# Decode attention on one core: VectorE products and sums over half heads instead of quarters, softmax totals once per four heads

## The chip, the cores and the metric

The kernel runs on one core of one Trainium2 chip. The metric is the device time of the whole program in microseconds (us), lower is better, as the median of several executions. The profile is one further execution; its span is about 1.8 us shorter than the time, so spans are compared with spans and times with times.

## The reference

One decoding step for four sequences: a layer norm, attention of 32 heads over the last 2048 positions of a cache, a gated FFN, and a sum.

```python
B, D, H, Dh, F = 4, 640, 32, 192, 1536            # bf16; W = 2048 positions of 8192
xn = layernorm(x)
q  = (xn @ wq) per head                           # one query row per sequence and head
p  = softmax(q . k[:, :, -2048:, :] * Dh ** -0.5)
o  = p . v[:, :, -2048:, :]
out = x + concat(o) @ wo + (silu(xn @ w1) * (xn @ w3)) @ w2
```

Each head needs 3.15 MB of K and 3.15 MB of V and uses each element once. That is 201 MB of the 223 MB which the kernel reads.

## The kernel before

K of one head lies in SBUF as 128 partitions (32 groups of positions x 4 sequences) x 64 positions x 192. A score is a dot product of length 192. The kernel forms it in three steps per *quarter* of a head (16 of the 64 positions): VectorE multiplies K by the query, TensorE adds six slices of 32 columns with an identity matrix into PSUM, VectorE sums the last 32. Then come a maximum over the head (VectorE, a TensorE transpose, VectorE again), exp on ScalarE, a masked copy `z` of the weights, and the PV matmuls.

```python
    def mult(u):                                   # u counts quarters: h, g = u // 4, u % 4
        pr = ppool.tile([P, JQ, Dh], BF16, tag="pr")
        nc.vector.tensor_tensor(out=pr[:], in0=kts[h][:, g * JQ:(g + 1) * JQ, :],
                                in1=qbc[...].to_broadcast([P, JQ, Dh]), op=ALU.mult)
        # ... (cut: bookkeeping)
    def adder(u):
        # ... (cut: the tiles ps and pr)
        for kk in range(NK):                       # 6 matmuls, 512 columns
            nc.tensor.matmul(ps[:], lhsT=idb[:], rhs=pr[:, :, kk * DD:(kk + 1) * DD], ...)
    def reduce_quarter(u):
        nc.vector.tensor_reduce(out=scs[h][:, g * JQ:(g + 1) * JQ], in_=pss.pop(u)[:], ...)
    def ge_tot(h):                                 # softmax total of one head, every head
        nc.tensor.matmul(po[sl, Dh:Dh + 1], lhsT=tot_w[...], rhs=rsums.pop(h)[:], ...)
```

The program is written as a table of (slot, phase, step). Within an engine the program records the instructions in exactly this order, and the traces show one whose input is late holding up those behind it: in the changed kernel the last 12 sums on TensorE start at 511.04 us, though their product is ready at 505.66, because a PV ahead of them waits for its z until 509.63. One slot is one quarter.

```python
    ends = {H - 2: (NU - 1, NU), H - 1: (NU + 3, NU + 4)}   # PV and fp32 sum of the last two heads
    for h in range(H):
        u0, ul = h * GQ, h * GQ + GQ - 1
        if h >= KBUFS: add((h - KBUFS + 1) * GQ, 0, load_k, h)
        if h < H - 2:  add(u0 + 2, 0, load_v, h)
        for u in range(u0, ul + 1):
            add(u, 1, mult, u); add(u + 1, 2, adder, u); add(u + 1, 8, reduce_quarter, u)
        add(ul + 1, 9, chain_lmax, h)               # VectorE: maximum per partition
        add(ul + 2, 3, chain_tr, h)                 # TensorE: transpose
        add(ul + 2, 4, chain_gmax, h)               # VectorE: maximum per sequence
        add(ul + 3, 3, chain_bc, h)                 # TensorE: broadcast; ScalarE: exp
        add(ul + 3, 4, chain_z, h)                  # VectorE: z
        add(ul + 4, 5, ge_tot, h)
        v, m = ends.get(h, (u0 + L, u0 + L + 1))
        add(v, 7, pv, h); add(m, 7, ge_sum, h)      # TensorE: PV; fp32 sum of its parts
        # ... (cut: once per four heads, the reciprocal of the totals and the turning of the output)
    # ... (cut: after K of head 31 the queue still loads V 30, V 31, w2 pieces, wo, w2 pieces)
```

## Time and profile before

| | value | where it is read |
|---|---|---|
| time | 525.69 us (525.55 to 526.71) | executions |
| span of the profiled run | 523.8 us | page |
| loads | 222.96 MB, load queue 99.2% of 16 engines | page, queue table |
| VectorE (DVE) / TensorE (PE) busy | 340.9 / 361.8 us | page |
| VectorE idle until a K tile came | 104.0 us | groups |

First the page of the kernel before: the span, then the span in 40 slices (DMA in tenths of full use, and what it moved).

```profile
span 523.8 us, 4820 instructions
...
DMA  9999999999999999999999999999999999999996
GB/s 389 422 443 425 433 431 432 428 433 432 430 435 428 437 418 446 424 437 426 434 434 429 432 434 429 435 427 435 425 437 434 427 437 431 430 434 425 441 418 275
```

The DMA row reads 9 (90% or more) in 39 of 40 slices and the rate is flat near 432 GB/s in the middle. No compute engine passes 70%. So the middle of the run is bound by bytes, and only the two ends can move.

The groups of the same kernel: line, engine, operation, output<-inputs, count | busy us, mean ns of one | idle us of the engine just before, and what ended it.

```profile
L277 DVE TENSOR_TENSOR pr<-kt,qbc 128x3072 bf16<-128x3072 bf16 x128 | 223.5, 1746 | 104.0 <-DMA kt<-in_A_k_cache_dram 104.0
L296 DVE TENSOR_REDUCE sc<-ps 128x16 f32<-128x512 f32 x128 | 87.1, 681 | 2.7 <-PE ps L288 2.6
...
L332 DVE TENSOR_TENSOR z<-ex,mask_b 128x256 bf16<-128x256 bf16 x32 | 13.5, 423 | 38.6 <-ACT ex L324 38.6
```

VectorE waits 104.0 us for K tiles, 3.3 us per head: it is ahead of the loads. Next, the chain that ended last, in order of time (start us, us, what).

```profile
489.68 30.66 DMA w<-in_B_w_dram
520.38 0.76 PE acc L264 x8
```

The end hangs on the last pieces of w2. Finally the end of the run in the timeline (start us, us, engine, line, operation).

```profile
496.99 1.76 DVE L277 TENSOR_TENSOR pr<-kt,qbc 128x3072 bf16<-128x3072 bf16 x1 [4.05 <-DMA kt<-in_A_k_cache_dram]
...
506.11 1.75 DVE L277 TENSOR_TENSOR pr<-kt,qbc 128x3072 bf16<-128x3072 bf16 x1
...
509.41 0.69 DVE L296 TENSOR_REDUCE sc<-ps 128x16 f32<-128x512 f32 x1 [0.95 <-PE ps L288]
...
512.82 0.42 DVE L332 TENSOR_TENSOR z<-ex,mask_b 128x256 bf16<-128x256 bf16 x1 [1.47 <-ACT ex L324]
...
513.30 2.71 PE L340 MATMUL o_ps<-vt,z 128*8 128x384 bf16 x32 [0.24 <-DVE z L332]
...
518.65 0.38 DVE L369 STREAM_TRANSPOSE oT<-og 128x192 bf16<-128x192 bf16 x1
...
520.38 0.71 PE L264 MATMUL acc<-w,hT 128*4 128x320 bf16 x8 [0.19 <-DMA w<-in_B_w_dram]
```

The last K tile is multiplied from 496.99 us, the last product ends at 507.86, the last sum at 510.10, the last z starts at 512.82, the last attention output is turned at 518.65, and the last w2 matmuls wait for DMA until 520.38. The work of the last head and the last load end within about 0.2 us of each other (its projection ends at 519.21 + 0.98 = 520.19).

### The profile page before, as it was taken

To read this page: it belongs to the slowest core of one execution; us is meant where nothing else is said; L and a number is where in the kernel's file an instruction comes from. 1 tells how busy PE (TensorE), PEld (TensorE's weight loads), DVE (VectorE), ACT (ScalarE), POOL (GpSimd) and SP (SyncE) were. 2 spreads that over 40 slices of the span, in tenths; PEclk is the share of its full clock that TensorE was granted. 3 is DMA by queue.
4 is the path that set the end of the run, shared out by engine and by line. 5 is a ranking of instruction groups with operands and counts; after the bars stand their busy time and mean duration, and the time that the engine had idled before them with its cause. 6 is when DMAs were issued, how large, how long until landed. Compare 5 with 4: busy or idle time off the path is not lost.

```text
span 523.8 us, 4820 instructions
## 1 busy us (share of the span) xinstructions
PE 361.8 (69%) x2336; PEld 75.9 (14%) x1643; DVE 340.9 (65%) x413; ACT 55.8 (11%) x176; POOL 5.6 (1%) x12
## 2 busy tenths in 40 slices
PE   0965866887668776667547768586686876675685
PEld 0100111121111111111111111111111111111122
DVE  3268853687656767577646877466667766667671
ACT  2111111111001110101100111001101110011111
POOL 4000000000000000000000000000000000000000
PEclk9979886898878998789997988889878898889988
DMA  9999999999999999999999999999999999999996
GB/s 389 422 443 425 433 431 432 428 433 432 430 435 428 437 418 446 424 437 426 434 434 429 432 434 429 435 427 435 425 437 434 427 437 431 430 434 425 441 418 275
DMA packets 11904, 223.26 MB, mean 426 GB/s; under 512 B 1332, under 2 KB 1608, under 8 KB 3052
## 3 DMA queue, kind: packets, MB, share of 16 engines
q1 hardware_dynamic: 11868, 222.96, 99.2%
q8 instruction: 15, 0.25, 0.2%
q14 instruction: 5, 0.04, 0.0%
q10 hardware_dynamic: 16, 0.01, 0.0%
HBM read 222.96 MB, written 0.01 MB: 426 GB/s over the span
## 4 chain that ended last, share of the span: by engine, by line
DMA 60%; PE 20%; DVE 15%; ACT 3%; issue 1%; SPq 1%
DMA kt<-in_A_k_cache_dram 44%; PE ps L288 11%; DMA w<-in_B_w_dram 11%; DVE pr L277 10%; DMA vt<-in_A_v_cache_dram 5%; PE po L361 4%; PE qps L243 3%; DVE sc L296 2%; ACT ex L324 1%; DVE z L332 1%; DMA x_sb<-in_A_x_dram 1%; PE mt L318 1%; ACT L324 0%; ACT negm L321 0%; PE mt L305 0%
## 5 line engine op out<-in xcount | busy, mean ns | idle before, releaser
L288 PE MATMUL ps<-pr,idb 128*128 128x512 bf16 x768 | 214.7, 422 | 137.6 <-DVE pr L277 137.5
L277 DVE TENSOR_TENSOR pr<-kt,qbc 128x3072 bf16<-128x3072 bf16 x128 | 223.5, 1746 | 104.0 <-DMA kt<-in_A_k_cache_dram 104.0
L296 DVE TENSOR_REDUCE sc<-ps 128x16 f32<-128x512 f32 x128 | 87.1, 681 | 2.7 <-PE ps L288 2.6
L340 PE MATMUL o_ps<-vt,z 128*8 128x384 bf16 x1024 | 60.5, 380 | 0.2 <-DVE z L332 0.2
L361 PE MATMUL po<-o_sb,sel_w 128*32 128x192 f32 x128 | 49.2, 518 | 0.6 <-ACT o_sb L343 0.6
L340 PEld LDWEIGHTS <-z 128*8 128x8 bf16 x1024 | 26.2, 95 | 98.8 <-issue 89.2
L332 DVE TENSOR_TENSOR z<-ex,mask_b 128x256 bf16<-128x256 bf16 x32 | 13.5, 423 | 38.6 <-ACT ex L324 38.6
L343 ACT COPY o_sb<-o_ps 128x384 f32<-128x384 f32 x32 | 15.3, 478 | 196.9 <-PE o_ps L340 196.9
L313 ACT ACTIVATE gneg<-gmax 1x128 f32<-1x128 f32 x32 | 9.8, 308 | 162.8 <-DVE gmax L310 162.8
L305 PEld LDWEIGHTS mt<-idf,lmax 128*1 128x1 f32 x32 | 3.2, 101 | 127.5 <-issue 125.5
L361 PEld LDWEIGHTS po<-o_sb,sel_w 128*32 128x32 f32 x128 | 13.8, 130 | 29.4 <-issue 27.9
L288 PEld LDWEIGHTS <-idb 128*128 128x128 bf16 x124 | 12.0, 97 | 39.3 <-issue 32.8
L318 PEld LDWEIGHTS mt<-ones_ff,gneg 1*128 1x128 f32 x64 | 9.6, 186 | 47.1 <-issue 43.7
L243 PE MATMUL qps<-wt,xnT 128*128 128x512 bf16 x59 | 14.9, 412 | 0.1
L318 PE MATMUL mt<-ones_ff,gneg 1*128 1x1 f32 x64 | 12.3, 259 | 0.7 <-ACT gneg L313 0.7
L321 ACT COPY negm<-mt 128x1 f32<-128x1 f32 x32 | 5.1, 159 | 70.4 <-PE mt L318 70.4
L310 DVE TENSOR_REDUCE gmax<-mt 1x4 f32<-1x128 f32 x32 | 8.8, 274 | 5.8 <-PE mt L305 5.8
L348 PEld LDWEIGHTS po<-rsum,tot_w 128*32 128x32 f32 x64 | 4.4, 108 | 51.5 <-ACT ex L324 35.4
L249 DVE CAST qbc<-qps 128x512 bf16<-128x512 f32 x6 | 3.8, 684 | 11.7 <-PE qps L243 11.7
L324 ACT ACTIVATE ex<-sc,negm 128x64 bf16<-128x64 f32 x32 | 11.1, 348 | 1.0
L305 PE MATMUL mt<-idf,lmax 128*1 128x128 f32 x32 | 10.9, 340 | 0.0
L199 PE MATMUL xnT_ps<-idb,xn 4*128 4x4 bf16 x5 | 0.4, 178 | 13.4 <-DVE xn L194 13.4
(74 smaller groups left out, 84.4 us busy)
## 6 DMA issues: line engine op xcount, KB each, us to landing
kt<-in_A_k_cache_dram SPq DMA_DIRECT2D x32, 3072.0 KB, 19.1
vt<-in_A_v_cache_dram SPq DMA_DIRECT2D x32, 3072.0 KB, 25.5
wo_t<-in_A_wo_dram SPq DMA_DIRECT2D x8, 960.0 KB, 20.7
wt<-in_A_wq_dram SPq DMA_DIRECT2D x2, 3072.0 KB
w<-in_B_w_dram SPq DMA_DIRECT2D x1, 1920.0 KB
wt<-in_A_wq_dram SPq DMA_DIRECT2D x1, 1536.0 KB, 19.5
w<-in_B_w_dram SPq DMA_DIRECT2D x1, 1536.0 KB
w<-in_B_w_dram SPq DMA_DIRECT2D x2, 640.0 KB
```

What stands on the lines that cost most here:

```text
L243: nc.tensor.matmul(qp[:], lhsT=xnT[:, kc].rearrange("p a b -> p (a b)"), rhs=wq_rows[kc][:, (c0 + i) * QC:(c0 + i + 1) * QC], start=(kc == ...
L277: nc.vector.tensor_tensor(out=pr[:], in0=kts[h][:, g * JQ:(g + 1) * JQ, :], in1=qbc[:, h * Dh:(h + 1) * Dh].unsqueeze(1).to_broadcast([P, ...
L288: nc.tensor.matmul(ps[:], lhsT=idb[:], rhs=pr[:, :, kk * DD:(kk + 1) * DD], start=(kk == 0), stop=(kk == NK - 1))
L296: nc.vector.tensor_reduce(out=scs[h][:, g * JQ:(g + 1) * JQ], in_=pss.pop(u)[:], axis=AX.X, op=ALU.add)
L305: nc.tensor.transpose(out=mt[0:1, 0:P], in_=chs[h][0][:], identity=idf[:])
L313: nc.scalar.activation(out=gneg[:], in_=gmax[:].unsqueeze(1).to_broadcast([1, PB, B]), func=ACTF.Copy, scale=-SCALE)
L318: nc.tensor.matmul(mt[:, P:P + 1], lhsT=gneg[:].rearrange("o p b -> o (p b)"), rhs=ones_ff[:], start=True, stop=True)
L324: nc.scalar.activation(out=ex[:], in_=scs.pop(h)[:], func=ACTF.Exp, bias=negm[:, 0:1], scale=SCALE, accum_out=rsum[:])
L332: nc.vector.tensor_tensor(out=z[:], in0=ex[:].unsqueeze(2).to_broadcast([P, NJ, B]), in1=mask_b[:].unsqueeze(1).to_broadcast([P, NJ, B]), ...
L340: nc.tensor.matmul(o_ps[c * CT:c * CT + 2 * B, :], lhsT=z[:, 2 * jj:2 * jj + 2, :], rhs=vt[:, 2 * jj:2 * jj + 2, :], start=(jj < 4), stop= ...
L343: nc.scalar.copy(out=o_sb[:], in_=o_ps[:])
L361: nc.tensor.matmul(po[sl, 0:Dh], lhsT=sel_w[:, par].rearrange("p a b -> p (a b)"), rhs=o_sb[:, par * Dh:(par + 1) * Dh].rearrange("p (r i) ...
```

## The change

The intent: save a fixed cost per VectorE instruction by doing the products and sums in half as many, twice as long; let TensorE do 12 sums in a row; form the softmax totals once per four heads with one matmul; and take the preparation of the FFN's input off the path to the first query. One sum now takes twice the PSUM (128x1024 fp32 instead of 128x512), and other PSUM pools are merged. The core of the diff (cut: the moved FFN preparation, constants moved to GpSimd, merged PSUM pools):

```diff
-    PBUFS: int = 4,
+    PBUFS: int = 2,
@@ mult
-        pr = ppool.tile([P, JQ, Dh], BF16, tag="pr")
-        nc.vector.tensor_tensor(out=pr[:], in0=kts[h][:, g * JQ:(g + 1) * JQ, :], ...
+        pr = ppool.tile([P, 2 * JQ, Dh], BF16, tag="pr")
+        nc.vector.tensor_tensor(out=pr[:], in0=kts[h][:, g * JQ:(g + 2) * JQ, :], ...
@@ adder
-        ps = ps_add.tile([P, JQ, DD], FP32, tag="ps")
+        ps = ps_add.tile([P, 2, JQ, DD], FP32, tag="ps")
-        for kk in range(NK):
-            nc.tensor.matmul(ps[:], lhsT=idb[:], rhs=pr[:, :, kk * DD:(kk + 1) * DD],
+        for i in range(2):
+            for kk in range(NK):
+                nc.tensor.matmul(ps[:, i], lhsT=idb[:], rhs=pr[:, i * JQ:(i + 1) * JQ, kk * DD:(kk + 1) * DD],
@@ schedule
-        for u in range(u0, ul + 1):
+        for u in range(u0, ul, 2):
             add(u, 1, mult, u)
-            add(u + 1, 2, adder, u)
-            add(u + 1, 8, reduce_quarter, u)
+            add(u + 2, 2, adder, u)
+            add(u + 2, 8, reduce_pair, u)
-        add(ul + 4, 5, ge_tot, h)
         if h % HG == HG - 1:
+            add(ul + 4, 4, ge_mask, h // HG)        # VectorE product, new
+            add(ul + 4, 5, ge_tot, h // HG)         # one matmul for four heads
             add(ul + 4, 9, ge_rec, h // HG)
```

More of the change, by code (lines that the diff above doesn't have):

```diff
@@ L111 @@
     ps_o = ctx.enter_context(tc.tile_pool(name="ps_o", bufs=2, space=MemoryType.PSUM))
-    ps_m = ctx.enter_context(tc.tile_pool(name="ps_m", bufs=1, space=MemoryType.PSUM))
-    ps_t = ctx.enter_context(tc.tile_pool(name="ps_t", bufs=1, space=MemoryType.PSUM))
     ps_po = ctx.enter_context(tc.tile_pool(name="ps_po", bufs=1, space=MemoryType.PSUM))
@@ L120 @@
     kts, vts, prs, pss, scs, exs, zs = {}, {}, {}, {}, {}, {}, {}
-    wos, o_sbs, rsums, rts, chs, oTs = {}, {}, {}, {}, {}, {}
+    wos, o_sbs, rsums, rws, rts, chs, oTs = {}, {}, {}, {}, {}, {}, {}
     def load_k(h):
@@ L157 @@
     make_identity(nc, idf[:])
-    ones_ff = const.tile([1, 1], FP32, name="ones_ff")
-    nc.vector.memset(ones_ff[:], 1.0)
+    ones_ff = const.tile([P, 1], FP32, name="ones_ff")
+    nc.gpsimd.memset(ones_ff[:], 1.0)
     mask_f = const.tile([P, B], FP32, name="mask_f")
@@ L163 @@
     mask_b = const.tile([P, B], BF16, name="mask_b")
-    nc.vector.tensor_copy(out=mask_b[:], in_=mask_f[:])
+    nc.gpsimd.tensor_copy(out=mask_b[:], in_=mask_f[:])
     rows = const.tile([P, 2 * B], FP32, name="rows")
@@ L170 @@
     tot_w = head.tile([P, NREP, B], FP32, name="tot_w")
-    nc.vector.tensor_copy(out=tot_w[:], in_=mask_f[:].unsqueeze(1).to_broadcast([P, NREP, B]))
+    nc.gpsimd.tensor_copy(out=tot_w[:], in_=mask_f[:].unsqueeze(1).to_broadcast([P, NREP, B]))
     sel_w = const.tile([P, 2, NREP, B], FP32, name="sel_w")
     for par in range(2):
-        nc.vector.tensor_copy(out=sel_w[:, par], in_=rows[:, par * B:(par + 1) * B].unsqueeze(1).to_broadcast([P, NREP, B]))
+        nc.gpsimd.tensor_copy(out=sel_w[:, par], in_=rows[:, par * B:(par + 1) * B].unsqueeze(1).to_broadcast([P, NREP, B]))
     xf = ppool.tile([B, D], FP32, tag="pr")
@@ L194 @@
     nc.vector.tensor_scalar_mul(out=xn[:], in0=xc[:], scalar1=rstd[:, 0:1])
-    xnT_ps = ps_t.tile([P, KC, B], BF16, tag="t")
+    xnT_ps = ps_add.tile([P, KC, B], BF16, tag="ps")
     for kc in range(KC):
@@ L208 @@
     assert D - LB == 5 * LP + LI and F % LE == 0
-    xm = ppool.tile([B, 2, PH, 2], BF16, tag="pr", name="xm")
-    nc.gpsimd.memset(xm[:], 0.0)
-    for i in range(2):
-        nc.vector.tensor_copy(out=xm[:, i, :, i], in_=xn[:, KM * P:LB])
-    xe = ppool.tile([B, 3 + LE, LF], BF16, tag="pr", name="xe")
-    nc.gpsimd.memset(xe[:], 0.0)
-    for g in range(2):
-        b0 = LB + g * 2 * LP
-        nc.vector.tensor_copy(out=xe[:, 0:2, g * CT:g * CT + LP].rearrange("b s (e i) -> b s e i", i=LI),
-                              in_=xn[:, b0:b0 + 2 * LP].rearrange("b (i e s) -> b s e i", e=LE, s=2))
@@ L219 @@
-    nc.vector.tensor_copy(out=xe[:, 2, 0:LP].rearrange("b (e i) -> b e i", i=LI),
-                          in_=xn[:, LB + 4 * LP:LB + 5 * LP].rearrange("b (i e) -> b e i", e=LE))
-    for e in range(LE):
-        nc.vector.tensor_copy(out=xe[:, 3 + e, CT + e * LI:CT + (e + 1) * LI], in_=xn[:, LB + 5 * LP:D])
-    NX = KM + 2
-    xw_ps = ps_t.tile([P, NX + 3 + LE, B], BF16, tag="t", name="xw_ps")
-    for kc in range(KM):
-        nc.tensor.transpose(out=xw_ps[:, kc, :], in_=xn[:, kc:KM * P:KM], identity=idb[0:B, 0:B])
@@ L227 @@
-    for i in range(2):
-        nc.tensor.transpose(out=xw_ps[:, KM + i, :], in_=xm[:, i].rearrange("b r h -> b (r h)"), identity=idb[0:B, 0:B])
-    for i in range(3 + LE):
-        nc.tensor.transpose(out=xw_ps[0:LF, NX + i, :], in_=xe[:, i, :], identity=idb[0:B, 0:B])
-    xw = const.tile([P, NX, NREP, B], BF16, name="xw")
-    nc.vector.tensor_copy(out=xw[:], in_=xw_ps[:, 0:NX, :].unsqueeze(2).to_broadcast([P, NX, NREP, B]))
-    xl = const.tile([LF, 3 + LE, NREP, B], BF16, name="xl")
-    nc.vector.tensor_copy(out=xl[:], in_=xw_ps[0:LF, NX:, :].unsqueeze(2).to_broadcast([LF, 3 + LE, NREP, B]))
@@ L237 @@
     qbc = const.tile([P, H * Dh], BF16, name="qbc")
     for c0 in range(0, NQ, 6):
-        qps = [pool.tile([P, QC], FP32, tag=tag, name="qps")
-               for pool, tag in ((ps_add, "ps"), (ps_add, "ps"), (ps_o, "o_ps"), (ps_o, "o_ps"), (ps_m, "mt"), (ps_t, "t"))]
+        pairs = [ps_add.tile([P, 2, QC], FP32, tag="ps", name="qps") for _ in range(2)]
+        qps = [pair[:, i, :] for pair in pairs for i in range(2)]
+        qps += [ps_o.tile([P, QC], FP32, tag="o_ps", name="qps")[:] for _ in range(2)]
@@ L241 @@
         for kc in range(KC):
             for i, qp in enumerate(qps):
-                nc.tensor.matmul(qp[:], lhsT=xnT[:, kc].rearrange("p a b -> p (a b)"),
+                nc.tensor.matmul(qp, lhsT=xnT[:, kc].rearrange("p a b -> p (a b)"),
                                  rhs=wq_rows[kc][:, (c0 + i) * QC:(c0 + i + 1) * QC],
@@ L248 @@
             if i % 2:
-                nc.vector.tensor_copy(out=dst, in_=qp[:])
+                nc.vector.tensor_copy(out=dst, in_=qp)
             else:
-                nc.scalar.copy(out=dst, in_=qp[:])
+                nc.scalar.copy(out=dst, in_=qp)
     o_banks = []
@@ L268, in acc_add @@
             acc_half(i, lhsT, rhs, last=last)
-    po = ps_po.tile([P, Dh + 1], FP32, name="po")
+    po_mt = ps_po.tile([P, Dh + 1 + P + 1], FP32, name="po_mt")
+    po, mt = po_mt[:, 0:Dh + 1], po_mt[:, Dh + 1:]
     def x_add(i):
@@ L275, in mult, with reduce_pair @@
         h, g = u // GQ, u % GQ
-        pr = ppool.tile([P, JQ, Dh], BF16, tag="pr")
-        nc.vector.tensor_tensor(out=pr[:], in0=kts[h][:, g * JQ:(g + 1) * JQ, :],
-                                in1=qbc[:, h * Dh:(h + 1) * Dh].unsqueeze(1).to_broadcast([P, JQ, Dh]),
+        pr = ppool.tile([P, 2 * JQ, Dh], BF16, tag="pr")
+        nc.vector.tensor_tensor(out=pr[:], in0=kts[h][:, g * JQ:(g + 2) * JQ, :],
+                                in1=qbc[:, h * Dh:(h + 1) * Dh].unsqueeze(1).to_broadcast([P, 2 * JQ, Dh]),
                                 op=ALU.mult)
         prs[u] = pr
-        if g == GQ - 1:
+        if g == GQ - 2:
             kts.pop(h)
     def adder(u):
-        ps = ps_add.tile([P, JQ, DD], FP32, tag="ps")
+        ps = ps_add.tile([P, 2, JQ, DD], FP32, tag="ps")
         pr = prs.pop(u)
-        for kk in range(NK):
-            nc.tensor.matmul(ps[:], lhsT=idb[:], rhs=pr[:, :, kk * DD:(kk + 1) * DD],
-                             start=(kk == 0), stop=(kk == NK - 1))
+        for i in range(2):
+            for kk in range(NK):
+                nc.tensor.matmul(ps[:, i], lhsT=idb[:], rhs=pr[:, i * JQ:(i + 1) * JQ, kk * DD:(kk + 1) * DD],
+                                 start=(kk == 0), stop=(kk == NK - 1))
         pss[u] = ps
-    def reduce_quarter(u):
+    def reduce_pair(u):
         h, g = u // GQ, u % GQ
@@ L295, in reduce_quarter @@
             scs[h] = small.tile([P, NJ], FP32, tag="sc", name="sc")
-        nc.vector.tensor_reduce(out=scs[h][:, g * JQ:(g + 1) * JQ], in_=pss.pop(u)[:], axis=AX.X, op=ALU.add)
+        nc.vector.tensor_reduce(out=scs[h][:, g * JQ:(g + 2) * JQ], in_=pss.pop(u)[:].rearrange("p i j d -> p (i j) d"),
+                                axis=AX.X, op=ALU.add)
     def chain_lmax(h):
@@ L303, in chain_tr @@
     def chain_tr(h):
-        mt = ps_m.tile([P, P + 1], FP32, tag="mt")
         nc.tensor.transpose(out=mt[0:1, 0:P], in_=chs[h][0][:], identity=idf[:])
-        chs[h].append(mt)
     def chain_gmax(h):
         gmax = small.tile([1, B], FP32, tag="gmax")
-        nc.vector.tensor_reduce(out=gmax[:], in_=chs[h][1][0:1, 0:P].rearrange("o (p b) -> o b p", b=B),
+        nc.vector.tensor_reduce(out=gmax[:], in_=mt[0:1, 0:P].rearrange("o (p b) -> o b p", b=B),
                                 axis=AX.X, op=ALU.max)
@@ L316, in chain_bc @@
     def chain_bc(h):
-        lmax, mt, gneg = chs[h]
-        nc.tensor.matmul(mt[:, P:P + 1], lhsT=gneg[:].rearrange("o p b -> o (p b)"), rhs=ones_ff[:],
+        lmax, gneg = chs.pop(h)
+        nc.tensor.matmul(mt[:, P:P + 1], lhsT=gneg[:].rearrange("o p b -> o (p b)"), rhs=ones_ff[0:1, :],
                          start=True, stop=True)
@@ L321, in chain_bc @@
         nc.scalar.copy(out=negm[:], in_=mt[:, P:P + 1])
-        rsum = small.tile([P, 1], FP32, tag="rsum", bufs=4)
+        if h % HG == 0:
+            rsums[h // HG] = small.tile([P, HG], FP32, tag="rsum", bufs=2, name="rsum")
         ex = small.tile([P, NJ], BF16, tag="ex")
         nc.scalar.activation(out=ex[:], in_=scs.pop(h)[:], func=ACTF.Exp, bias=negm[:, 0:1], scale=SCALE,
-                             accum_out=rsum[:])
-        rsums[h] = rsum
+                             accum_out=rsums[h // HG][:, h % HG:h % HG + 1])
         exs[h] = ex
@@ L344, in pv, with ge_mask, ge_tot @@
         o_sbs[h] = o_sb
-    def ge_tot(h):
-        sl = slice((h % HG) * CT, (h % HG + 1) * CT)
-        nc.tensor.matmul(po[sl, Dh:Dh + 1], lhsT=tot_w[:].rearrange("p a b -> p (a b)"), rhs=rsums.pop(h)[:],
+    def ge_mask(hg):
+        rw = small.tile([P, HG, CT], FP32, tag="rw", bufs=1, name="rw")
+        nc.vector.tensor_tensor(out=rw[:], in0=tot_w[:].rearrange("p a b -> p (a b)").unsqueeze(1).to_broadcast([P, HG, CT]),
+                                in1=rsums.pop(hg)[:].unsqueeze(2).to_broadcast([P, HG, CT]), op=ALU.mult)
+        rws[hg] = rw
+    def ge_tot(hg):
+        nc.tensor.matmul(po[:, Dh:Dh + 1], lhsT=rws.pop(hg)[:].rearrange("p h c -> p (h c)"), rhs=ones_ff[:],
                          start=True, stop=True)
-        chs.pop(h)
     def ge_rec(hg):
@@ L382, with w1_rows, w1_x @@
     ffn = {}
+    NX = KM + 2
+    xw = const.tile([P, NX, NREP, B], BF16, name="xw")
+    xl = const.tile([LF, 3 + LE, NREP, B], BF16, name="xl")
+    xs = {}
+    def w1_rows():
+        xm = small.tile([B, 2, PH, 2], BF16, tag="xm", bufs=1, name="xm")
+        nc.gpsimd.memset(xm[:], 0.0)
+        for i in range(2):
+            nc.gpsimd.tensor_copy(out=xm[:, i, :, i], in_=xn[:, KM * P:LB])
+        xe = small.tile([B, 3 + LE, LF], BF16, tag="xe", bufs=1, name="xe")
+        nc.gpsimd.memset(xe[:], 0.0)
+        for g in range(2):
+            b0 = LB + g * 2 * LP
+            nc.gpsimd.tensor_copy(out=xe[:, 0:2, g * CT:g * CT + LP].rearrange("b s (e i) -> b s e i", i=LI),
+                                  in_=xn[:, b0:b0 + 2 * LP].rearrange("b (i e s) -> b s e i", e=LE, s=2))
+        nc.gpsimd.tensor_copy(out=xe[:, 2, 0:LP].rearrange("b (e i) -> b e i", i=LI),
+                              in_=xn[:, LB + 4 * LP:LB + 5 * LP].rearrange("b (i e) -> b e i", e=LE))
+        for e in range(LE):
+            nc.gpsimd.tensor_copy(out=xe[:, 3 + e, CT + e * LI:CT + (e + 1) * LI], in_=xn[:, LB + 5 * LP:D])
+        xs.update(m=xm, e=xe)
+    def w1_x():
+        xm, xe = xs["m"], xs["e"]
+        xw_ps = ps_add.tile([P, NX + 3 + LE, B], BF16, tag="ps", name="xw_ps")
+        for kc in range(KM):
+            nc.tensor.transpose(out=xw_ps[:, kc, :], in_=xn[:, kc:KM * P:KM], identity=idb[0:B, 0:B])
+        for i in range(2):
+            nc.tensor.transpose(out=xw_ps[:, KM + i, :], in_=xm[:, i].rearrange("b r h -> b (r h)"), identity=idb[0:B, 0:B])
+        for i in range(3 + LE):
+            nc.tensor.transpose(out=xw_ps[0:LF, NX + i, :], in_=xe[:, i, :], identity=idb[0:B, 0:B])
+        nc.vector.tensor_copy(out=xw[:], in_=xw_ps[:, 0:NX, :].unsqueeze(2).to_broadcast([P, NX, NREP, B]))
+        nc.vector.tensor_copy(out=xl[:], in_=xw_ps[0:LF, NX:, :].unsqueeze(2).to_broadcast([LF, 3 + LE, NREP, B]))
     FM, FH = KM * F, KM * F + F // 2
@@ L408, in w1_in @@
         wt, we = ffn["w1"], ffn["w1e"]
-        ps = ffn["ps"] = ps_t.tile([P, FW], FP32, tag="t", name="f_ps")
+        ps = ffn["ps"] = ps_add.tile([P, FW], FP32, tag="ps", name="f_ps")
         def mm(w, lhsT, rhs, c0=0, start=False, stop=False):
@@ L442, in w3_in @@
     def w3_in():
-        ffn["ps"] = ps_t.tile([P, FW], FP32, tag="t", name="f_ps")
+        ffn["ps"] = ps_add.tile([P, FW], FP32, tag="ps", name="f_ps")
         for kc in range(KC):
@@ L511 @@
         add(4 + 2 * n, 1, w1_low, n)
+    add(5, 0, w1_rows)
+    add(9, 7, w1_x)
     add(13, 7, w1_in)
```

## The prediction

> **What bounds the kernel now.** The bytes. The page's DMA row reads 9 in 39 of 40 slices; the queue table gives the load queue 99.2% of 16 engines' span. [...] the middle slices move 418 to 446, about 432 on average[...]. DVE is busy 340.9 us (65%), PE 361.8 us (69%): neither binds. DVE waits 104.0 us for K tiles and PE 137.5 us for products (groups). A K load is issued 19.1 us (median) before it lands, though 3 MB need 7.3 us: some 12 us of other loads are queued ahead, so compute may slip several us without idling DMA.
>
> Only the ends are not hidden. The timeline shows a balanced finish: the last head's projection ends at 520.2 us, the last w2 piece is waited for until 520.38, then come 0.7 us of matmuls, a 0.5 us cast and about 2.2 us of output.
>
> **What the change does, costed.**
> - Product: 128 of 1746 ns become 64. [...] Estimate 3.35 us each, saving 9 us.
> - Sum: 128 of 681 ns become 64 of about 1.21 us, saving 9.5 us.
> - Totals: 32 fp32 matmul pairs become 8, minus 5 us of PE; 8 small DVE products added.
> - Start: eight small DVE copies (1.1 us) and 12 transposes (0.75 us of PE) leave the path to q. K work starts 0.5-1 us earlier; loads are queued then, so nothing is gained.
>
> DVE busy should fall to about 323-327 us. None of this is on the critical path while loads saturate DMA: value about 0 us. DMA should end near 520 us and the last K tile land near 497.0 us, as now.
>
> **The tail is what moves.** From that landing, chains are coarser. Before: landing 497.0, last z starts 512.8. Estimate after, from durations of this trace: product 500.35; preceding head's sum 501.5, maximum and transpose 502.9 (DVE now stands still for it, 0.7 us); second product 506.2; PE does the previous o sums (1.5 us) and 12 matmuls (2.6 us, more if cold: the clock was 0.50 at 500-502 us after 3.6 us idle, and this idle gets longer) to 506.6-508; z to 508.5-509.7; PV 1.5 us; only then the last 12 matmuls, to 512.8-514; sum 1.2 us; then the 2.7 us chain: z at 516.8-518, 4-5 us later. The totals now wait for a DVE product and stand before the last PV: another 0.4 us. Slack against DMA is 0.2 us.
>
> **Predicted: 529.5 us** (+0.7%), 8 in 10 between 526.0 and 532.5. Faster by over 2%: 1%; within 2%: 96%; slower by over 2%: 3%.
>
> **What would show it.** Right: middle slices stay near 432 GB/s; products x64 near 3.35 us, sums x64 near 1.21 us; the last z starts at 516-519 us; the last w2 matmuls wait for PE or DVE, no longer for DMA; 5 to 9 us between the last load's landing and the end, instead of 3.5. Wrong: z still near 513 us, or the last matmuls still released by DMA.
>
> **What would make it wrong.** Clock at the tail: cold 12-matmul groups (0.427 us each) would add 2-3 us; a warm tail could save as much. [...] Coarser groups could starve the queue if waits exceed the 12 us cushion; I think not.

Passages are cut where marked: a ceiling of the load rate, a gain of up to 3 us set against it, and the derivation of the product's 3.35 us from an element rate and a fixed cost. 3.35 us, and the 1.21 us for the sum, stand as estimates (3342 and 1217 ns were measured). 9 and 9.5 us saved on VectorE take its 340.9 us to about 322, and with the 8 small products added 323 to 327 was stated; for the time z 4 to 5 us later plus 0.4 us for the totals less 0.2 us of slack come to about 530 to 531 us, and 529.5 was stated. The gain of up to 3 us stood among the risks, outside that sum.

## The result, and the profile after

| | before | after |
|---|---|---|
| time, median of 5 | 525.69 us (525.55 to 526.71) | 531.19 us (530.56 to 531.71) |
| span of the profiled run | 523.8 us | 529.1 us |
| VectorE busy / TensorE busy | 340.9 / 361.8 us | 334.0 / 358.3 us |
| VectorE idle until a K tile came | 104.0 us | 33.2 us |
| mean granted TensorE clock | 0.892 | 0.858 |

The ratio is 1.0101 (95% interval 1.0087 to 1.0116). Ratios here are the mean time of one kernel's runs over that of the other's of the same rounds, so they are not quite the ratio of the medians quoted. The change makes the kernel 5.5 us slower, clear of noise.

The page of the changed kernel, the same rows:

```profile
span 529.1 us, 4580 instructions
...
DMA  9999999999999999999999999999999999999992
GB/s 385 433 429 431 436 431 428 433 431 430 434 429 431 436 431 424 442 425 434 430 437 427 436 419 435 437 431 430 431 434 429 437 430 431 431 430 437 425 422 105
```

The middle slices carry the same rate, 431 or 432 GB/s over each of the stretches from 100 us to 480 us, as before. What differs is the last slice: 105 GB/s instead of 275. The loads end when they did (issue plus time to landing of the 480 KB piece of w2: 520.3 us, in both), and then the core works on without loading, for 8.8 us instead of 3.5. The groups:

```profile
L249 DVE TENSOR_TENSOR pr<-kt,qbc 128x6144 bf16<-128x6144 bf16 x64 | 213.8, 3342 | 33.3 <-DMA kt<-in_A_k_cache_dram 33.2
...
L269 DVE TENSOR_REDUCE sc<-ps 128x32 f32<-128x1024 f32 x64 | 77.9, 1217 | 6.4 <-PE ps L261 6.4
...
L304 DVE TENSOR_TENSOR z<-ex,mask_b 128x256 bf16<-128x256 bf16 x32 | 13.5, 423 | 86.5 <-ACT ex L297 86.5
```

The halves cost what was expected, 3342 and 1217 ns. TensorE's sums are as many as before. Yet VectorE's wait for K shrank to 33.2 us although it is busy for less: it is closer behind the loads, not further ahead. It now waits 86.5 us (38.6 before) for the exp that precedes z. The chain that ended last:

```profile
496.92 3.36 DVE pr L249
...
504.06 4.09 PE ps L261 x12
...
511.11 2.71 PE ps L261 x12
...
518.76 2.69 PE o_ps L312 x32
...
523.58 2.83 PE acc L235 x34
```

No DMA is left in the chain after 496.92 us: TensorE's sums and PV bind where the load of w2 bound before. The timeline of the same stretch:

```profile
496.92 3.36 DVE L249 TENSOR_TENSOR pr<-kt,qbc 128x6144 bf16<-128x6144 bf16 x1 [0.23 <-DMA kt<-in_A_k_cache_dram]
...
502.32 3.34 DVE L249 TENSOR_TENSOR pr<-kt,qbc 128x6144 bf16<-128x6144 bf16 x1
...
502.54 1.52 PE L337 MATMUL po_mt<-o_sb,sel_w 128*32 128x192 f32 x4 [0.46 <-DVE gmax L282]
...
503.99 4.16 PE L261 MATMUL ps<-pr,idb 128*128 128x512 bf16 x12
...
509.15 0.43 DVE L304 TENSOR_TENSOR z<-ex,mask_b 128x256 bf16<-128x256 bf16 x1 [3.50 <-ACT ex L297]
...
509.63 1.47 PE L312 MATMUL o_ps<-vt,z 128*8 128x384 bf16 x32 [1.18 <-DVE z L304]
...
511.04 2.76 PE L261 MATMUL ps<-pr,idb 128*128 128x512 bf16 x12
...
513.84 1.23 DVE L269 TENSOR_REDUCE sc<-ps 128x32 f32<-128x1024 f32 x1 [3.12 <-PE ps L261]
...
517.43 0.42 DVE L304 TENSOR_TENSOR z<-ex,mask_b 128x256 bf16<-128x256 bf16 x1 [1.47 <-ACT ex L297]
...
518.70 2.73 PE L312 MATMUL o_ps<-vt,z 128*8 128x384 bf16 x32
...
525.65 0.71 PE L235 MATMUL acc<-w,hT 128*4 128x320 bf16 x8
```

Read it against the one before. The last product ends at 505.66 us, 2.2 us *earlier* than before. But the last sum ends at 515.07, 5.0 us *later*. Between the two stands TensorE's queue, in its fixed order: four fp32 sums of head 29 (502.54), the 12 sums of head 31's first half at a low clock (4.16 us; granted clock 0.50 in 504 to 506 us, 0.79 in 506 to 508), a wait for z of head 30 (509.15), PV of head 30 (1.47 us), and only then the last 12 sums (511.04). That z is late because the broadcast which its exp needs stands behind the first 12 sums on TensorE and starts only at 508.08 us. The 5.3 us of span divide like this: z starts 4.6 us later; PV starts 1.27 us after z instead of 0.48, because the new product and matmul of the totals stand between (0.8 us); from there to the end the two kernels differ by 0.1 us.

### The profile page after: what moved, and what is told of

Its sections match the earlier page's. It is cut to its first block, busy times and chain, and to the rows that moved or that the text cites. A ratio compares the mean times of both kernels' runs of the same rounds, so it can differ in the third digit from the quotient of the medians.

```text
span 529.1 us, 4580 instructions
## 1 busy us (share of the span) xinstructions
PE 358.3 (68%) x2289; PEld 65.5 (12%) x1534; DVE 334.0 (63%) x280; ACT 55.9 (11%) x176; POOL 7.5 (1%) x25
## 4 chain that ended last, share of the span: by engine, by line
DMA 56%; DVE 27%; PE 14%; ACT 1%; issue 1%; SPq 0%
DMA kt<-in_A_k_cache_dram 50%; DVE pr L249 18%; DMA w<-in_B_w_dram 5%; PE ps L261 5%; DVE sc L269 4%; PE po_mt L337 3%; PE qps L214 3%; DMA x_sb<-in_A_x_dram 1%; PE o_ps L312 1%; PE po_mt L278 1%; DVE gmax L282 1%; DVE lmax L274 1%; PE acc L235 1%; DVE qbc L220 0%; DVE og L342 0%
## 5 line engine op out<-in xcount | busy, mean ns | idle before, releaser
L249 DVE TENSOR_TENSOR pr<-kt,qbc 128x6144 bf16<-128x6144 bf16 x64 | 213.8, 3342 | 33.3 <-DMA kt<-in_A_k_cache_dram 33.2
L269 DVE TENSOR_REDUCE sc<-ps 128x32 f32<-128x1024 f32 x64 | 77.9, 1217 | 6.4 <-PE ps L261 6.4
L278 PE MATMUL po_mt<-idf,lmax 128*1 128x128 f32 x32 | 9.9, 311 | 105.0 <-DVE lmax L274 104.9
L304 DVE TENSOR_TENSOR z<-ex,mask_b 128x256 bf16<-128x256 bf16 x32 | 13.5, 423 | 86.5 <-ACT ex L297 86.5
L337 PE MATMUL po_mt<-o_sb,sel_w 128*32 128x192 f32 x128 | 48.7, 515 | 14.1 <-DVE gmax L282 13.4
L312 PE MATMUL o_ps<-vt,z 128*8 128x384 bf16 x1024 | 50.8, 333 | 1.2 <-DVE z L304 1.2
L290 PEld LDWEIGHTS po_mt<-ones_ff,gneg 1*128 1x128 f32 x64 | 9.4, 182 | 112.5 <-issue 111.6
L293 ACT COPY negm<-po_mt 128x1 f32<-128x1 f32 x32 | 5.1, 159 | 163.4 <-PE po_mt L290 163.4
L337 PEld LDWEIGHTS po_mt<-o_sb,sel_w 128*32 128x32 f32 x128 | 14.0, 130 | 36.5 <-issue 33.9
L282 DVE TENSOR_REDUCE gmax<-po_mt 1x4 f32<-1x128 f32 x32 | 8.9, 279 | 15.1 <-PE po_mt L278 15.1
L290 PE MATMUL po_mt<-ones_ff,gneg 1*128 1x1 f32 x64 | 12.1, 256 | 0.7 <-ACT gneg L285 0.7
## 6 DMA issues: line engine op xcount, KB each, us to landing
wt<-in_A_wq_dram SPq DMA_DIRECT2D x1, 1536.0 KB, 19.8
```

The lines of the kernel that those rows point to most:

```text
L269: nc.vector.tensor_reduce(out=scs[h][:, g * JQ:(g + 2) * JQ], in_=pss.pop(u)[:].rearrange("p i j d -> p (i j) d"), axis=AX.X, op=ALU.add)
L278: nc.tensor.transpose(out=mt[0:1, 0:P], in_=chs[h][0][:], identity=idf[:])
L282: nc.vector.tensor_reduce(out=gmax[:], in_=mt[0:1, 0:P].rearrange("o (p b) -> o b p", b=B), axis=AX.X, op=ALU.max)
L290: nc.tensor.matmul(mt[:, P:P + 1], lhsT=gneg[:].rearrange("o p b -> o (p b)"), rhs=ones_ff[0:1, :], start=True, stop=True)
L304: nc.vector.tensor_tensor(out=z[:], in0=ex[:].unsqueeze(2).to_broadcast([P, NJ, B]), in1=mask_b[:].unsqueeze(1).to_broadcast([P, NJ, B]), ...
L312: nc.tensor.matmul(o_ps[c * CT:c * CT + 2 * B, :], lhsT=z[:, 2 * jj:2 * jj + 2, :], rhs=vt[:, 2 * jj:2 * jj + 2, :], start=(jj < 4), stop= ...
```

## The experiments

The theory: **the loss lies in the last two heads**. All other work hides behind the loads, but what follows the last K tile does not, and there coarser groups make TensorE's queue longer between the last product and the last z. Rival 1: half heads cost something all along the run, for instance by the lower mean clock. Rival 2: the other parts of the change (totals, FFN preparation, PSUM pools) cost it. All kernels gave correct results. Each was timed in five rounds beside the kernel before, on the same chip; the medians of the kernel before in the three groups of four, four and three, and the last single run, were 525.69, 525.87, 525.63 and 525.78 us. The groups ran on different chips, and the changed kernel itself was timed only once, before them; so where a text below says how much of the 5.5 us came back, it compares across groups, and the ratio to the kernel before is the firmer number.

### 1. Which heads? Three kernels

The changed kernel gets a switch per head for the number of quarters that one group covers.

```diff
+    def NQH(h):
+        return 1 if (CONDITION) else 2
     # mult, adder and the sum take NQH(h) quarters; the schedule steps by NQH(h)
+        n = NQH(h)
+        for u in range(u0, ul + 1, n):
+            add(u, 1, mult, u); add(u + n, 2, adder, u); add(u + n, 8, reduce_pair, u)
```

Quarters in heads 30 and 31 only:

> The changed kernel with only the last two heads (30 and 31) in quarters again; the other 30 heads stay in half heads. Tail theory (the loss lies between the landing of the last K tile and the last z, because the last heads' groups are coarse): nearly all of the 5.3 us comes back; span 523.8 to 525.0 us, the last z starts at 512.5 to 513.5 us instead of 517.4. Rival 1 (half heads cost something all along the run, for instance by the lower granted clock, 0.858 against 0.892): 30 of 32 heads still pay, so at most 0.4 us comes back. Rival 2 (the totals, the moved FFN preparation or the PSUM pools cost it): nothing comes back.

Measured: 527.06 us (525.47 to 527.65), ratio to before 1.0020 (1.0008 to 1.0032). 4.1 of the 5.5 us come back. In the profiled run, the slowest of the five, the span is 525.9 us and the last z starts at 514.30, over the expected ranges by 0.9 and 0.8 us: right in direction, not quite in size.

Quarters in heads 0 to 29, half heads in 30 and 31 only:

> The mirror: the changed kernel with heads 0 to 29 in quarters and only heads 30 and 31 in half heads. Tail theory: as slow as the changed kernel, span 528.3 to 529.6 us, last z at 517 to 518 us, and DVE busy back near 341 us with no effect on the time. Rival 1: about the time of the kernel before, 523.8 to 524.5. Rival 2: 529.

Measured: 530.37 us (528.59 to 532.09), ratio 1.0091 (1.0075 to 1.0108), span 528.5 us in the profiled run. With VectorE busy for 340.0 us, as long as before, the loss is nearly whole: two coarse heads out of 32 make 4.7 us (against the next kernel, all in quarters). The last z starts at 517.08 in the profiled run.

Quarters everywhere, so that only the other parts of the change remain:

> The changed kernel with all heads in quarters: what is left of the change is the totals once per four heads, the moved FFN preparation and the PSUM pools. Tail theory: the kernel before plus at most 0.5 us for the totals that stand before the last PV, span 523.8 to 524.6. Rival 2: 529.

Measured: 525.70 us, ratio 1.0001 (0.9989 to 1.0013). Rival 2 is out: totals, moved preparation and merged pools together cost nothing that can be seen while the end has room for them. Here the last 8 matmuls start at 520.56 us against 520.38 before.

Rival 1 is out as the main cause, but not quite to zero: half heads in the first 30 heads go with 1.4 us where the end is in quarters (527.06 against 525.70) and with 0.8 us where it is coarse (531.19 against 530.37), the second less than the spread of the runs. The profiled runs show how such a difference can arise: with half heads ahead of it, matmuls of the end took longer (12 of head 31's 24 sums 2.35 + 1.97 us, PV 2.73 us) than with quarters ahead (1.47 + 1.47 and 1.64), and the mean granted clock of the run was 0.864 against 0.912; the clock in that stretch alone was not read. That is one profile each, and the first is of the slowest run of its kernel (527.65 us; its fastest took 525.47, as little as the kernel before); the link is argued, not shown.

### 2. TensorE's order at the end

PV and fp32 sum of head 30 go behind the last 12 sums.

```diff
-    ends = {H - 2: (NU - 1, NU), H - 1: (NU + 3, NU + 4)}
+    ends = {H - 2: (NU, NU + 2), H - 1: (NU + 3, NU + 4)}
```

> The changed kernel with TensorE's order at the end mended: PV of head 30 and its fp32 sum come after the last 12 summing matmuls instead of before them. Tail theory: the last sums no longer stand behind PV 30 (1.5 us) and the transpose of head 31 no longer behind the fp32 sum (1.5 us); the last z starts some 2.5 us earlier, near 515 us, and the span falls by about as much, to 526 to 527.5 us. If the coarse VectorE groups alone make the loss, nothing changes.

Measured: 527.22 us (526.71 to 527.51), ratio 1.0020 (1.0006 to 1.0033): 4.0 us back with half heads in all 32 heads, by an edit of the order alone. The timeline of this kernel:

```profile
508.08 2.76 PE L261 MATMUL ps<-pr,idb 128*128 128x512 bf16 x12
...
510.88 1.22 DVE L269 TENSOR_REDUCE sc<-ps 128x32 f32<-128x1024 f32 x1 [0.47 <-PE ps L261]
...
514.56 0.42 DVE L304 TENSOR_TENSOR z<-ex,mask_b 128x256 bf16<-128x256 bf16 x1 [1.47 <-ACT ex L297]
```

That is more than the 2.5 us expected. The last 12 sums start at 508.08 us instead of 511.04, right behind the first 12, and z moves from 517.43 to 514.56, by 2.9 us. Not all of it is the waiting: the first 12 sums took 3.78 us here instead of 4.16, which leaves 2.5 us, as expected, and the last PV took 2.28 instead of 2.73 us. About 0.8 of the 3.6 us of span thus came through these shorter matmuls and not through the waiting (the granted clock of this stretch was not read). Still, a coarse VectorE group is not by itself most of the loss. Most of it is that a group of 12 sums has to stand behind something which in turn waits: PV of head 30 needs z of head 30, and the broadcast for that z stands behind the first 12 sums. With the order mended 1.4 us remain against the kernel before of the same rounds.

### 3. The clock at the end

Matmuls whose result nobody reads are put into two waits of TensorE, 44 after PV of head 29 and 20 after the broadcast of head 31.

```diff
+    def keep_warm(n):
+        for _ in range(n):
+            nc.tensor.matmul(spare, lhsT=idb[:], rhs=qbc[:, 0:128], start=True, stop=True)
+    add(NU - 4, 9, keep_warm, 44)
+    add(NU + 2, 5, keep_warm, 20)
```

> The changed kernel with matmuls that nobody reads put into two of TensorE's waits at the end (44 of 128 columns after PV of head 29, 20 after the broadcast of head 31), to keep its granted clock up. The output stays right. If the low clock is part of the loss: the 12 sums of head 31's first half take 2.8 us instead of 4.2 and the last PV 1.5 instead of 2.7, the span falls by 1.5 to 2.7 us, to 526.4 to 527.6. If the clock has no part: no change or up to 0.5 us slower.

Measured: 528.23 us (527.62 to 530.81), ratio 1.0047 (1.0027 to 1.0066): 3.0 us back by the median, though one of six runs stayed at 530.81. The timeline:

```profile
499.00 2.63 PE L246 MATMUL po_mt<-qbc,idb 128*128 128x128 bf16 x44
...
504.12 2.76 PE L266 MATMUL ps<-pr,idb 128*128 128x512 bf16 x12
...
517.17 1.48 PE L317 MATMUL o_ps<-vt,z 128*8 128x384 bf16 x32
```

Both targets moved as expected: 4.16 to 2.76 us for the sums, 2.73 to 1.48 for PV. 2.76 us is what the last 12 sums of the changed kernel took (511.04 us) at a granted clock of 1.00. In the changed kernel the stretch of those sums reads (the last three numbers are the granted clock, the DMA share and GB/s):

```profile
504.00:506.00 2.00, 2.00 (x6) 0.09 (x1) 1.66 (x1) 0.00 (x0) 0.00 (x0) 0.50 1.00 430
```

The granted clock reads 0.50 here, after TensorE had idled 3.28 us before 501.81. No run shows how long an idle time it takes: with only the order changed (experiment 2) TensorE idled longer there, 3.73 us, and the sums took less, 3.78 us. Whether the clock makes the spread between runs of one kernel is not shown either: it was 3.2 us here, and 0.6, 1.9, 0.4 and 1.8 us for the kernel before in its four groups of runs, but the changed kernel without these matmuls spread by only 1.2 us. The low clock is no cost that the change added from nothing, though: the last PV took 2.71 us in the kernel before as well, at a granted clock of 0.51 from 513.3 to 516 us.

### 4. The totals

The last group's totals are recorded behind the last PV.

```diff
-            add(ul + 4, 5, ge_tot, h // HG)
+            add(ul + 4, 8 if h == H - 1 else 5, ge_tot, h // HG)
```

> The changed kernel with one edit: in the last group the matmul of the totals is recorded after the last PV instead of before it. Tail theory: the last PV starts when z is written instead of after the totals' product and matmul, 0.6 to 0.9 us earlier, and the span falls by as much, to 528.2 to 528.6 us. If the totals cost nothing: no change.

Measured: 530.31 us (527.84 to 530.62), ratio 1.0080 (1.0066 to 1.0094): 0.9 us, as expected. The profiled run was the fastest of the six, and its first 12 sums of head 31 took 3.46 us instead of 4.16, so its span (526.0 us) does not show the edit alone.

### 5. The three edits together

> The changed kernel with the three edits that helped alone put together (PV 30 behind the last sums, last totals behind the last PV, unread matmuls in two waits), loads as they were. Tail theory: order gave 4.0 us, of which the three overlap; the z of head 31 starts near 513 us and the loads bind again, 525.4 to 526.3 us, with the spread of the runs back under 0.8 us. If something else of the change still costs time: 527 or more.

Measured: 526.15 us (526.04 to 526.42), ratio 1.0009 (0.9996 to 1.0022). 5.0 of the 5.5 us are back with half heads in every head and the loads untouched; 0.5 us remains, and the interval does not tell it from 0. The three alone sum to 7.9 us, more than there was to win, because they shorten the same stretch in part. In the profiled run z starts at 513.63, but the last projection still ends at 520.39 + 0.98 = 521.37 us, just behind the loads. The timeline shows why:

```profile
513.63 0.42 DVE L309 TENSOR_TENSOR z<-ex,mask_b 128x256 bf16<-128x256 bf16 x1 [1.47 <-ACT ex L302]
...
514.38 0.51 PE L342 MATMUL po_mt<-o_sb,sel_w 128*32 128x192 f32 x1
514.40 0.33 PE L317 MATMUL o_ps<-vt,z 128*8 128x384 bf16 x2
...
515.06 0.53 PE L342 MATMUL po_mt<-o_sb,sel_w 128*32 128x192 f32 x1
```

The granted clock is 1.00 in every stretch of 2 us from 492 to 524 us, so a low clock is not what remains. But the edit of section 2 put the fp32 sum of head 30 right before the last PV, and the 20 unread matmuls stand ahead of both: the four matmuls of that sum run from 514.38 to 515.94 us, PV runs among and behind them, and its 32 matmuls take from 514.40 to 517.23 (the last 24 of them 515.41 + 1.82), 2.83 us instead of the 1.48 of experiment 3. Moving that sum behind PV might give back up to 1.4 us of it (an estimate from these two durations); no run tried it.

### 6. Moving the last K tile forward: two misses

If everything hangs on the landing of K of head 31, an earlier landing should hide the chain. First, V of head 29 is issued behind that K.

```diff
-        if h < H - 2:
+        if h < H - 3:
             add(u0 + 2, 0, load_v, h)
-    for h in range(H - 2, H):
+    for h in range(H - 3, H):
         add(NU - 6, 0, load_v, h)
```

> The changed kernel with one load moved: V of head 29 is issued after K of head 31 instead of before it; the bytes and their total stay. The last K tile then lands some 7.3 us earlier (3 MB at 432 GB/s), near 489.7 us, and the loads still end near 520 us. Tail theory: the last z starts near 513 us, the loads bound the end again, span 523.6 to 524.8 us. If half heads cost something all along the run instead: no change, 529.

Measured: 530.33 us (529.44 to 531.03), ratio 1.0078 (1.0064 to 1.0093). Two things went wrong, and the trace shows both. The first is in the stretches of this kernel (busy us per engine, granted clock, DMA share, GB/s):

```profile
480.00:485.00 5.00, 3.84 (x38) 0.80 (x31) 5.00 (x4) 0.60 (x3) 0.00 (x0) 1.00 0.63 221
485.00:490.00 5.00, 2.49 (x23) 0.67 (x10) 4.51 (x5) 0.79 (x2) 0.00 (x0) 1.00 1.05 447
```

The K load has to wait for its buffer until 481.3 us, and with nothing else issued the queue ran dry: 221 GB/s in 480 to 485 us. (It then landed 10.1 us after its issue, near 491.4 instead of the 489.7 expected.) The second is in its timeline:

```profile
495.01 3.35 DVE L249 TENSOR_TENSOR pr<-kt,qbc 128x6144 bf16<-128x6144 bf16 x1
...
500.08 2.73 PE L312 MATMUL o_ps<-vt,z 128*8 128x384 bf16 x32 [4.56 <-DMA vt<-in_A_v_cache_dram]
...
502.75 0.37 PE L278 MATMUL po_mt<-idf,lmax 128*1 128x128 f32 x1
...
503.36 3.34 DVE L249 TENSOR_TENSOR pr<-kt,qbc 128x6144 bf16<-128x6144 bf16 x1
```

K of head 31 was used from 495.01 us, but PV of head 29 now waited for its late V tile until 500.08, the transpose of head 30 stood behind it on TensorE, and VectorE's second product stood behind that transpose's result: it started at 503.36, later than the 502.32 of the changed kernel. One late load was passed on by in-order queues, to TensorE and from there to VectorE.

The same move in the kernel before:

> The same move in the kernel before. Its end is bound by the last loads and not by the work after the last K tile, so an earlier last K tile buys at most the 0.2 us of slack plus part of the 0.7 us of last matmuls: span 523.2 to 524.0 us. If the chain from the last K tile bound it too: 3 us or more faster.

Measured: 526.71 us (525.81 to 528.07), ratio 1.0012 (0.9996 to 1.0028). No gain, as a DMA-bound end predicts, but also not the small gain expected; in the profiled run (525.4 us) the rate sags to 396 and 378 GB/s between 475 and 485 us.

Second try: keep the queue fed with two w2 pieces before that K, and take PV of heads 29 and 30 out of the way on TensorE.

```diff
+    for i in range(2):
+        add(NU - 10, 0, w2_load, i)
+    for h in range(H - 3, H):
+        add(NU - 6, 0, load_v, h)
-    ends = {H - 2: (NU - 1, NU), H - 1: (NU + 3, NU + 4)}
+    ends = {H - 3: (NU - 2, NU), H - 2: (NU + 2, NU + 3), H - 1: (NU + 3, NU + 4)}
     # and the last totals behind the last PV, as in 4
```

> The changed kernel, half heads everywhere, with the end rearranged: two w2 pieces (1.31 MB, 3 us) are issued before K of head 31, so the queue cannot run dry as it did when V of head 29 was moved alone (221 GB/s at 480 to 485 us); V of head 29 follows it; and on TensorE the PV of heads 29 and 30 and their fp32 sums stand behind the sums of head 31, the last totals behind the last PV. Tail theory: the last K lands near 493 us, the last z starts at 508 to 511 us, nothing after it binds, the last w2 matmuls are again released by DMA: 525.2 to 525.9 us, level with the kernel before, with half heads in all 32 heads. If half heads cost time along the run: still 1 us or more slower.

Measured: 527.37 us (526.28 to 528.68), ratio 1.0032 (1.0019 to 1.0045). 3.8 us better than the change, but not by an earlier start on K:

```profile
489.55 4.83 PE L261 MATMUL ps<-pr,idb 128*128 128x512 bf16 x12
...
495.39 0.43 DVE L304 TENSOR_TENSOR z<-ex,mask_b 128x256 bf16<-128x256 bf16 x1 [4.17 <-ACT ex L297]
...
496.87 3.35 DVE L249 TENSOR_TENSOR pr<-kt,qbc 128x6144 bf16<-128x6144 bf16 x1
...
515.38 0.43 DVE L304 TENSOR_TENSOR z<-ex,mask_b 128x256 bf16<-128x256 bf16 x1 [1.48 <-ACT ex L297]
```

The first product of head 31 starts at 496.87 us, as late as ever, and this time without a wait for DMA. VectorE had stood waiting for the exp of head 29 until 495.39 us, and that exp stood behind 12 sums of head 30 which TensorE ran at the low clock (4.83 us instead of 2.76; granted clock 0.50 to 0.56 from 488 to 494 us). The first 12 sums of head 31 then met the low clock too (5.33 us; 0.50 from 502 to 506 us). The last z starts at 515.38 instead of the 508 to 511 us expected. So the last K tile was *not* the only gate in the changed kernel; the chain of the two heads ahead of it was nearly as late. The profile after had said so: the product at 496.92 us waited for DMA for 0.23 us only, where the one before had waited 4.05 us. In the profiles of the other kernels with half heads at the end that wait is 0 to 1.2 us.

The same rearrangement in the kernel before:

> The same rearrangement of loads and PV in the kernel before, which is bound by DMA at its end already: 525.1 to 525.8 us, no difference that can be told from 0, at most 0.4 us faster because the last w2 piece alone then waits.

Measured: 526.58 us (526.32 to 527.00), ratio 1.0018 (1.0006 to 1.0030), so 0.9 us slower. PV of head 31 now waits for its V tile and starts at 514.48 us instead of 513.30, and the balanced end tips over: moving loads in a kernel whose ends meet within 0.2 us only shifts which of them is late.

### 7. A closing version

Half heads in heads 0 to 29, quarters in the last two, and the edits of 2, 3 and 4 (24 instead of 44 unread matmuls).

> The closing version: half heads in heads 0 to 29, quarters in heads 30 and 31, PV 30 behind the last sums, the last totals behind the last PV, 24 and 20 unread matmuls in two waits of the end. If order, grain and clock at the end are the whole loss: the projection of the last group is done before the last w2 piece lands, the loads bind again, 525.3 to 525.8 us, level with the kernel before and at most 0.4 us faster. If something along the run remains: 526.2 or more, as with the three edits in half heads (526.15).

Measured: 526.74 us (525.90 to 527.85), ratio 1.0021 (1.0005 to 1.0036). A miss. The runs fall in two groups, three at 525.9 to 526.1 and three at 527.4 to 527.9; the profile was of the first kind (525.99 us), and there six sums of the last head took 1.46 or 1.47 us, as at a granted clock of 1.00 in the kernel before (1.45 us at 507.92). Whether the others met a low clock there no profile shows. No version tried beats the kernel before.

## Why the prediction was right or wrong

- **The time: right.** 529.5 us was predicted with 526.0 to 532.5, and 531.19 was measured. The direction and size came from one step, the walk through the tail: z at 516.8 to 518 was forecast, 517.43 measured. The walk was even better than the number drawn from it: 4 to 5 us for z and 0.4 for the totals, less 0.2 of slack, make about 530 to 531 us, over the 529.5 stated. The experiments confirm that step from two sides: coarse groups in two heads alone make 4.7 us, and mending TensorE's order alone takes 4.0 us away, some of it by shorter matmuls. The last matmuls no longer waited for DMA, and 8.8 us lay between the landing of the 480 KB piece of w2 and the end (8.4 for the last piece of all); 5 to 9 were forecast.
- **"None of this is on the critical path while loads saturate DMA": right.** The middle moved at the same rate, and halving the number of instructions in 30 heads bought nothing (experiment 1).
- **Unit costs: right.** Products 3342 ns (3.35 us estimated), sums 1217 ns (1.21).
- **"DVE busy should fall to about 323-327 us": wrong.** It fell to 334.0. The forecast took durations for busy time. The durations did fall as estimated: summed over all VectorE records of the two traces, 363.5 to 343.7 us, by 19.8. But neighbours on VectorE overlap in the record, by about 80 ns in each pair that adjoins. Before there are 282 such pairs among 413 instructions, 22.5 us in all; after, 122 among 280, 9.7 us. Of the 145 to 150 ns of duration that each instruction saved was worth, some 80 were thus already hidden under the neighbour, and halving the number of instructions lowered the busy time by only 6.9 us.
- **"DVE now stands still for it, 0.7 us": right in kind, smaller.** 0.45 us at that place, and 15.1 us over all 32 heads (5.8 before).
- **"K work starts 0.5-1 us earlier": wrong, without consequence.** The first product starts at 32.86 us, against 32.25 before. The FFN preparation has left the path, but VectorE's copy of the queries now waits for ScalarE's copy (it starts at 29.86 instead of 29.25 us). Loads were queued, as the prediction says, so the time doesn't show it.
- **The cold clock: named as a risk of 2 to 3 us and met in part.** The first 12 sums took 4.16 us and ended at 508.15, at the late edge of the forecast. A longer idle time before them was forecast as the reason; it was 3.28 us (3.55 before), then one matmul of 0.27 us, then 0.46 us more. So it was not longer, and what set the clock is not shown. The unread matmuls took 3.0 us off by the median (experiment 3), part of it from a PV that was slow before too.
- **"The totals ... another 0.4 us": undersized.** PV starts 0.8 us later after z, and 0.9 us came back when they were moved.
- **"From that landing, chains are coarser": too simple.** It gave the right time because the landing and the chain of heads 29 and 30 came together, 0.23 us apart in this profile. That was luck: the prediction didn't work it out. But two experiments built on it failed: with an earlier landing, those heads still held TensorE and VectorE and with them the last head. The cushion of VectorE against K shrank from 104.0 to 33.2 us over the run, which I had not forecast.
- **Open:** the 0.8 to 1.4 us that half heads in the first 30 heads go with; a low clock at the end in some runs would explain them, but only the longer matmuls of single profiles speak for it (2.35 us against 1.47 for six sums, experiment 1). And the 0.5 us that the mended kernel may still lack: there the profile speaks against the clock (1.00 to the end) and for the fp32 sum before the last PV (experiment 5), untested.

## What to carry to other kernels

Here loads bound the middle (431 or 432 GB/s before and after), cutting instructions there bought no time, and the value of the regrouping was decided by what still had to run after the last large load. In a kernel like it, walk that stretch instruction by instruction, engine by engine, in program order. Larger groups saved 145 to 150 ns of duration per instruction but lengthened the serial path product, sum, maximum, exp, PV (z of the last head 4.6 us later), and on an engine that takes its work in order one late group became a queue; where a group stands in that queue was worth up to 4.0 us here, while the 6.9 us of VectorE time saved were worth none. And before moving loads to start the tail earlier, read what the first instruction of the tail really waited for: if it was 0.23 us of DMA, an earlier load alone can save hardly more than that (here, in experiment 6, the last z came 0.35 us earlier). Two more things measured: the length of TensorE's matmuls counted at the end, where no load hid it (unread matmuls took 3.0 us off by the median; with them 12 sums took 2.76 us, without them 4.16 at a granted clock of 0.50 to 0.79); and one load moved behind another that waited for its buffer cut the rate to 221 GB/s for 5 us.
